# Attention and expansion kernel: DMA transposes from tile 8, two load buffers, a later model of the loads, and the last rows summed in two halves

## Chip, cores and metric

The kernel runs on one core of one Trainium2 chip. The metric is device microseconds of that core. A time is the median of several runs. A ratio is the mean time of one kernel's fast runs over that of the other kernel's fast runs in the same rounds, so it is not quite the ratio of the medians quoted.

## The reference

Attention with a sliding window of 96 keys, 8 global keys and a linear position bias, then a two-layer network with a squared ReLU:

```python
# q, k, v: (4, 8, 768, 64), normal draws times 0.1
scores = scale * np.matmul(q, k.transpose(0, 1, 3, 2)) + bias    # bias = -slope * distance
scores = np.where(keep, scores, -1e9)
a = softmax(scores)
x = np.matmul(a, v)            # as (3072, 512)
out = np.maximum(x @ w_in, 0)**2 @ w_out     # (512, 2048), (2048, 512)
```

## The kernel before

The 3072 rows are 24 tiles of 128. For each tile q and k are loaded, cast to bf16 on the way, transposed, multiplied to scores, and so on to x, which is transposed again (`xT`). Two tiles make a block for the two layers (`hT`, `hs`, `acc`). A small planner (class `Plan`) takes operations with costs, dependences and buffers, and decides in which order they are written. A tracker then sets the semaphores: **each access waits for those written before it that touch the same tile.** The loads that GpSimd issues take eight completion semaphores in turn, called lanes below; each load that lands adds 16 to its lane, so a wait for 64 is a wait for the lane's fourth load.

Three places matter. The load buffers are a ring indexed by the tile's number:

```python
JQK, JX = 10, 10          # from these tiles on, q/k and x are transposed by DMA
NQ, NKT = 10, 2 * TPB
qk_ring = [const([P, 2, d_model], BF16, f"qk_{i}") for i in range(NQ)]

def load_part(n, j):
    swdge(("qk"[n], j), qk_ring[j % NQ][:, n, :].rearrange(...),
          src_rows((q, k)[n], j).rearrange(...), 0.85)
```

The loads of tiles 1 to 5 and of all weights are written at once, ahead of the plan; those from tile 6 on are operations of the plan, which wait for the readers of their buffer:

```python
load_part(0, 1); ...; load_part(1, 1); load_v(0); load_v(1)
for w in "i0 T2 i1 T3 i2 o0 i3 o1 i4 o2 T4 i5 o3 i6 o4 T5 i7 o5 o6 o7".split():
    kind, n = w[0], int(w[1:])
    {"T": load_tile, "i": load_w_in, "o": load_w_out}[kind](n)
...
for j in range(NT):
    if j in late:                          # late = range(6, 24)
        ld = plan.op(("load", j), {"POOLQ": 2.6}, emit_load,
                     deps=qk_users[j % NQ] + [ones[j]], ...)
    ...                                    # transposes of tile j, reading qk_ring[j % NQ]
```

And all matmuls, transposes among them, go through TensorE in the written order.

The softmax here doesn't subtract the row's maximum and nothing guards it: scores larger than these inputs give would overflow.

## Time and profile before

| what | value |
|---|---|
| time | 221.83 us, 3 runs, 221.41 to 222.29 |
| span of the profile | 220.5 us |
| first transpose of tile 1's q starts | 5.70 us |
| TensorE's waits for loads of q and k | 4.0 us |
| last matmul ends / span ends | 216.45 / 220.5 us |

In the profile's lines PE is TensorE, PEld its weight loads, DVE VectorE, ACT ScalarE, POOL GpSimd and SP SyncE. The DMA share in the ten-microsecond windows can read above 1; use it only to compare rows. The prediction below shows the lines it rests on. Beside them, the page's row of slices: 40 equal slices of the span, busy tenths of TensorE, its granted clock in tenths, and the busy share of the DMA engines.

```profile
PE   7779879799999999999999999999999999999992
PEclk9979999999999999999999999999999999999998
DMA  9999999999999999999542532531730620310211
```

TensorE is nearly full from the ninth slice on, and its only holes are in the first 46 us, while the DMA engines are full.

### The profile page before, as it was taken

To read this page: it belongs to the slowest core of one execution; us is meant where nothing else is said; L and a number is where in the kernel's file an instruction comes from. 1 tells how busy PE (TensorE), PEld (TensorE's weight loads), DVE (VectorE), ACT (ScalarE), POOL (GpSimd) and SP (SyncE) were. 2 spreads that over 40 slices of the span, in tenths; PEclk is the share of its full clock that TensorE was granted. 3 is DMA by queue.
4 is the path that set the end of the run, shared out by engine and by line. 5 is a ranking of instruction groups with operands and counts; after the bars stand their busy time and mean duration, and the time that the engine had idled before them with its cause. 6 is when DMAs were issued, how large, how long until landed. Compare 5 with 4: busy or idle time off the path is not lost.

```text
span 220.5 us, 5058 instructions
## 1 busy us (share of the span) xinstructions
PE 206.9 (94%) x1992; PEld 143.5 (65%) x2024; DVE 144.0 (65%) x372; ACT 122.5 (56%) x224; POOL 73.7 (33%) x91
## 2 busy tenths in 40 slices
PE   7779879799999999999999999999999999999992
PEld 3658658457667676676667667666667766766740
DVE  5456858647677786775668668666767768745520
ACT  3648865626846657545636736733845744724430
POOL 7997658797962996404000000000000000000000
PEclk9979999999999999999999999999999999999998
DMA  9999999999999999999542532531730620310211
GB/s 129 148 167 200 180 190 192 165 208 161 165 189 131 155 199 145 158 197 132 140 60 48 144 54 45 147 64 33 168 72 4 166 27 12 109 24 16 82 38 59
DMA packets 107304, 26.03 MB, mean 118 GB/s; under 512 B 97936, under 2 KB 104336, under 8 KB 107280
## 3 DMA queue, kind: packets, MB, share of 16 engines
q0 software_dynamic: 79200, 13.37, 82.3%
q1 hardware_dynamic: 28080, 12.33, 25.7%
q8 instruction: 16, 0.26, 0.5%
q14 instruction: 8, 0.07, 0.1%
HBM read 27.26 MB, written 6.29 MB: 152 GB/s over the span
## 4 chain that ended last, share of the span: by engine, by line
PE 77%; DMA 12%; POOL 6%; issue 2%; DVE 1%; ACT 0%; POOLq 0%
PE hT L652 34%; PE acc L716 34%; DMA wout<-in_moe_w_out_dram 4%; PE sc L428 4%; DMA win<-in_moe_w_in_dram 4%; PE po L541 4%; DMA qk<-in_q_dram 4%; POOL qk L189 2%; POOL v L189 2%; POOL win L189 1%; PE tr L370 1%; POOL wout L189 1%; PE trx L604 1%; DVE hs L685 0%; ACT hr L673 0%
## 5 line engine op out<-in xcount | busy, mean ns | idle before, releaser
L652 PE MATMUL hT<-xT,win 128*128 128x256 bf16 x768 | 99.0, 273 | 0.2
L716 PE MATMUL acc<-wout,hs 128*128 128x512 bf16 x352 | 91.5, 379 | 2.0 <-DVE hs L685 0.6
L673 ACT ACTIVATE hr<-hT 128x512 f32<-128x512 f32 x96 | 57.3, 597 | 55.6 <-PE hT L652 54.1
L652 PEld LDWEIGHTS <-win 128*128 128x128 bf16 x768 | 71.1, 98 | 16.7
L685 DVE TENSOR_TENSOR hs<-hr 128x512 bf16<-128x512 f32 x96 | 65.0, 689 | 23.3 <-ACT hr L673 22.5
L716 PEld LDWEIGHTS <-hs 128*128 128x128 bf16 x384 | 36.6, 98 | 29.1 <-DVE hs L685 1.2
L474 ACT ACTIVATE esc<-sc 128x512 bf16<-128x512 f32 x78 | 42.3, 599 | 14.7 <-PE sc L428 14.7
L499 DVE TENSOR_TENSOR at<-esc,E 128x512 bf16<-128x512 bf16 x78 | 32.7, 421 | 8.6 <-ACT esc L474 7.2
L189 POOL DMA_DIRECT2D qk<-in_q_dram x23 | 20.8, 904 | 14.8 <-DMA qkT<-qk 9.0
L189 POOL DMA_DIRECT2D v<-in_v_dram x24 | 21.5, 896 | 7.6 <-DVE at L499 2.7
L189 POOL DMA_DIRECT2D qk<-in_k_dram x23 | 20.6, 897 | 2.8 <-DMA v<-in_v_dram 2.1
L569 DVE TENSOR_TENSOR x<-po,rs 128x256 bf16<-128x256 f32 x48 | 20.4, 424 | 1.7
L541 PEld LDWEIGHTS <-at 128*128 128x128 bf16 x352 | 16.7, 98 | 4.8
L541 PE MATMUL po<-v,at 128*128 128x65 bf16 x352 | 18.5, 193 | 0.0
L428 PEld LDWEIGHTS <-qkT 64*128 64x128 bf16 x352 | 10.0, 95 | 10.9 <-issue 8.0
L568 DVE RECIPROCAL rs<-po 128x4 f32<-128x4 f32 x48 | 8.5, 178 | 10.9 <-PE po L541 10.8
L428 PE MATMUL sc<-qkT 64*128 64x128 bf16 x192 | 13.4, 221 | 1.7 <-ACT qkT L300 0.9
L300 ACT COPY o<-acc 128x512 f32<-128x512 f32 (+1 forms) x15 | 8.4, 573 | 9.2 <-PE acc L716 8.3
L302 DVE COPY o<-acc 128x512 f32<-128x512 f32 (+1 forms) x10 | 6.6, 664 | 9.6 <-PE acc L716 5.0
L428 PE MATMUL sc<-qkT,qkT 64*128 64x128 bf16 x160 | 11.6, 218 | 0.0
L370 PE MATMUL tr<-ident,qk 128*128 128x128 bf16 x72 | 6.8, 225 | 4.0 <-DMA qk<-in_q_dram 2.1
L370 PEld LDWEIGHTS <-qk 128*128 128x128 bf16 x72 | 4.9, 101 | 6.1 <-DMA qk<-in_q_dram 3.0
(40 smaller groups left out, 72.9 us busy)
## 6 DMA issues: line engine op xcount, KB each, us to landing
out_dram<-o SPq DMA_DIRECT2D x23, 256.0 KB, 2.7
v<-in_v_dram POOLq DMA_DIRECT2D x24, 128.0 KB, 7.6
qk<-in_q_dram POOLq DMA_DIRECT2D x23, 128.0 KB, 7.4
qk<-in_k_dram POOLq DMA_DIRECT2D x23, 128.0 KB, 7.7
win<-in_moe_w_in_dram POOLq DMA_DIRECT2D x8, 256.0 KB, 8.1
wout<-in_moe_w_out_dram POOLq DMA_DIRECT2D x8, 256.0 KB, 8.8
plain<-in_q_dram SPq DMA_DIRECT2D x1, 256.0 KB, 3.2
plain<-in_k_dram SPq DMA_DIRECT2D x1, 256.0 KB, 3.9
```

Of the source, the lines that this page charges most:

```text
L189: nc.gpsimd.dma_start(out=dst, in_=src)
L370: nc.tensor.transpose(out=tr[:, pair, :], in_=src[:, pair * P : (pair + 1) * P], identity=ident32 if fp else ident,)
L428: nc.tensor.matmul(out=sc[odd, g][:, at, :], lhsT=qkT[(j - kt) % NKT][half, 1, pair, :], rhs=qkT[j % NKT][half, 0, pair, :], start=True, s ...
L474: nc.scalar.activation(out=esc, in_=tiles.pop(("sc", j, odd, g)).rearrange("p a c -> p (a c)"), func=Act.Exp, scale=scale,)
L499: nc.vector.tensor_mul(at, tiles.pop(("esc", j, odd, g)), bias)
L541: nc.tensor.matmul(out=po[:, hi, :], lhsT=tiles["at", j, odd, g][:, at * P : (at + 1) * P], rhs=v_sb[kj][:, h, :], start=(i == 0), stop=(i ...
L568: nc.vector.reciprocal(rs, po[:, :, D : D + 1])
L569: nc.vector.tensor_tensor(out=x[:, 4 * hf : 4 * hf + 4, :], in0=po[:, :, :D], in1=rs.to_broadcast([P, 4, D]), op=Alu.mult,)
L652: nc.tensor.matmul(out=hT[:, c, :], lhsT=w_in_sb[s][:, kt, c * P : (c + 1) * P], rhs=tiles["xT", blk][:, kt, :], start=(kt == 0), stop=(kt ...
L673: nc.scalar.activation(hr, tiles.pop(("hT", blk, s)), Act.Relu)
L685: nc.vector.tensor_mul(hs, hr, hr)
L716: nc.tensor.matmul(out=tiles["acc", blk, sub], lhsT=hs[:, c, sub * P : (sub + 1) * P], rhs=w_out_sb[s][:, c, :], start=(s == 0 and c == 0) ...
```

## The change

Its intent: less TensorE work (transposes of tiles 8 and 9 go to DMA), less memory (two load buffers, each load just in time), a planner that knows better when loads land, and a shorter end. Its core:

```diff
-    LAG = {..., "SP": 2.6, "POOLQ": 2.5, "DMA": 0.0}
+    LAG = {..., "SP": 2.6, "POOLQ": 0.8, "DMAQ": 1.2, "DMA": 0.0}
-    JQK, JX = 10, 10
-    NQ, NKT = 10, 2 * TPB
+    JQK, JX = 8, 8
+    NQ, NKT = 2, 2 * TPB
-        land[name] = issue[1] + 0.3
+        land[name] = issue[1] + 0.3 + min(max(0.1 * (issue[1] - 8), 0.0), 1.6)
+            ld = plan.op(("data", j), {"DMAQ": 2.7}, None, deps=[ld], key=base)
...
+        parts = [(0, None), (1, 0), (1, 1)] if last else [(0, None), (1, None)]
...          # the second half of the last rows has an accumulator of its own:
+                    pool, tag = (ps_g, "g") if own else (ps_acc, "acc")
+                    tiles["acc", blk, sub, half] = pool.tile([P, w], FP32, name="acc", tag=tag)
-                        rhs=w_out_sb[s][:, c, :],
+                        rhs=w_out_sb[s][:, c, cols],
...          # and both halves are copied out by ScalarE
```

More of the change, by code (lines that the diff above doesn't have):

```diff
@@ L22 @@
 class Plan:
-    LAG = {"PE": 0.25, "ACT": 0.15, "DVE": 0.12, "SP": 2.6, "POOLQ": 2.5, "DMA": 0.0}
+    LAG = {"PE": 0.25, "ACT": 0.15, "DVE": 0.12, "SP": 2.6, "POOLQ": 0.8, "DMAQ": 1.2, "DMA": 0.0}
     URGE = 0.05
@@ L701, with emit_s2 @@
         last = blk == NBLK - 1
-        acc_users = [[], []]
+        acc_users = {}
+        parts = [(0, None), (1, 0), (1, 1)] if last else [(0, None), (1, None)]
         order2 = (
-            [(s, sub) for sub in range(2) for s in range(NSTEP)]
+            [(s, *p) for p in parts for s in range(NSTEP)]
             if last
-            else [(s, sub) for s in range(NSTEP) for sub in range(2)]
+            else [(s, *p) for s in range(NSTEP) for p in parts]
         )
-        for s, sub in order2:
-            users = acc_users[sub]
-            def emit_s2(e, blk=blk, s=s, sub=sub):
+        for s, sub, half in order2:
+            users = acc_users.setdefault((sub, half), [])
+            w = d_model if half is None else d_model // 2
+            cols = slice(0, w) if half is None else slice(half * w, (half + 1) * w)
+            own = half == 1
+            def emit_s2(e, blk=blk, s=s, sub=sub, half=half, w=w, cols=cols, own=own):
                 if s == 0:
-                    tiles["acc", blk, sub] = ps_acc.tile([P, d_model], FP32, name="acc", tag="acc")
+                    pool, tag = (ps_g, "g") if own else (ps_acc, "acc")
+                    tiles["acc", blk, sub, half] = pool.tile([P, w], FP32, name="acc", tag=tag)
                 hs = tiles["hs", blk, s]
@@ L716, in emit_s2 @@
                     nc.tensor.matmul(
-                        out=tiles["acc", blk, sub],
+                        out=tiles["acc", blk, sub, half],
                         lhsT=hs[:, c, sub * P : (sub + 1) * P],
-                        rhs=w_out_sb[s][:, c, :],
+                        rhs=w_out_sb[s][:, c, cols],
                         start=(s == 0 and c == 0),
@@ L726 @@
             o = plan.op(
-                ("s2", blk, s, sub), {"PE": 0.43}, emit_s2,
+                ("s2", blk, s, sub), {"PE": 0.43 * w / d_model}, emit_s2,
                 deps=[d, land["wout", s]] + users[-1:],
-                key=8 * blk + s + 2.0 + (50 if last and sub else 0),
-                takes=("acc", NACC, [users]) if s == 0 else None,
+                key=8 * blk + s + 2.0 + (0 if not last else 8 * sub + 8 * (half or 0)),
+                takes=((*G, [users]) if own else ("acc", NACC, [users])) if s == 0 else None,
             )
@@ L734 @@
             if s == NSTEP - 1:
-                for half in (0, 1) if last and sub == 1 else (None,):
-                    cols = (
-                        slice(None)
-                        if half is None
-                        else slice(half * d_model // 2, (half + 1) * d_model // 2)
-                    )
-                    ousers = []
-                    def emit_o(e, blk=blk, sub=sub, half=half, cols=cols):
-                        o_sb = work.tile([P, d_model], FP32, name="o", tag="o", bufs=4)
-                        any_copy(e, o_sb[:, cols], tiles["acc", blk, sub][:, cols])
-                        tiles["o", blk, sub, half] = o_sb
-                    costs = {"ACT": 0.57, "DVE": 0.62}
-                    if half is not None:
-                        costs = [{"ACT": 0.4}, {"DVE": 0.35}][half]
-                    ev = plan.op(
-                        ("o", blk, sub), costs, emit_o, deps=[o], key=8 * blk + s + 1.0,
-                        takes=("o", 4, [ousers]),
-                    )
-                    users.append(ev)
-                    ousers.append(ev)
-                    def emit_st(e, blk=blk, sub=sub, half=half, cols=cols):
-                        r0 = (blk * 2 + sub) * P
-                        nc.sync.dma_start(
-                            out=out[r0 : r0 + P, cols],
-                            in_=tiles.pop(("o", blk, sub, half))[:, cols],
-                        )
-                    st = plan.op(
-                        ("st", blk, sub), {"SP": 0.4}, emit_st, deps=[ev],
-                        key=8 * blk + s + 9.0,
-                    )
-                    ousers.append(st)
@@ L772, with emit_o @@
-    for o in plan.run({"PE": 4.2, "DVE": 4.4, "ACT": 4.2}):
+                ousers = []
+                def emit_o(e, blk=blk, sub=sub, half=half, cols=cols):
+                    o_sb = work.tile([P, d_model], FP32, name="o", tag="o", bufs=4)
+                    any_copy(e, o_sb[:, cols], tiles["acc", blk, sub, half])
+                    tiles["o", blk, sub, half] = o_sb
+                ev = plan.op(
+                    ("o", blk, sub), {"ACT": 0.57, "DVE": 0.62} if half is None else {"ACT": 0.37},
+                    emit_o, deps=[o], key=8 * blk + s + 1.0, takes=("o", 4, [ousers]),
+                )
@@ new lines, with emit_st @@
+                users.append(ev)
+                ousers.append(ev)
+                def emit_st(e, blk=blk, sub=sub, half=half, cols=cols):
+                    r0 = (blk * 2 + sub) * P
+                    nc.sync.dma_start(
+                        out=out[r0 : r0 + P, cols],
+                        in_=tiles.pop(("o", blk, sub, half))[:, cols],
+                    )
+                st = plan.op(
+                    ("st", blk, sub), {"SP": 0.4}, emit_st, deps=[ev],
+                    key=8 * blk + s + 9.0,
+                )
@@ L773 @@
+                ousers.append(st)
+    for o in plan.run({"PE": 4.2, "DVE": 4.4, "ACT": 4.2, "DMAQ": issue[1]}):
         if o["emit"]:
```

## The prediction

> **What bounds the kernel now.** I read the ten-microsecond windows first, because the page's "PE 94%" is an average over stages. Columns: stretch, its length, then busy microseconds of TensorE, its weight loads, VectorE, ScalarE and GpSimd, the granted TensorE clock, the DMA share and GB/s.
>
> ```profile
> 0.00:10.00 10.00, 7.47 (x78) 4.65 (x79) 4.92 (x28) 4.57 (x8) 8.87 (x15) 1.00 1.37 137
> 10.00:20.00 10.00, 8.21 (x114) 6.91 (x113) 5.57 (x35) 6.03 (x14) 8.56 (x12) 0.83 1.87 178
> 20.00:30.00 10.00, 8.11 (x99) 5.68 (x100) 7.52 (x22) 7.56 (x17) 6.44 (x9) 1.00 1.63 189
> ...
> 50.00:60.00 10.00, 9.89 (x94) 6.93 (x94) 6.64 (x15) 6.90 (x14) 8.76 (x11) 1.00 2.43 156
> ```
>
> From about 46 us on every window but the last has 9.9 of 10 us busy on TensorE: whatever delays TensorE is added to the end, and only removed TensorE work is gained. Only the first 46 us have holes. The timeline of TensorE shows them: start, length, instruction, and in brackets the idle time and who ended it.
>
> ```profile
> 5.70 0.39 PE L370 MATMUL tr<-ident,qk 128*128 128x128 bf16 x4
> ...
> 11.90 0.40 PE L370 MATMUL tr<-ident,qk 128*128 128x128 bf16 x4 [1.01 <-DMA qk<-in_q_dram]
> 12.79 0.40 PE L370 MATMUL tr<-ident,qk 128*128 128x128 bf16 x4 [0.50 <-DMA qk<-in_k_dram]
> ...
> 26.36 0.39 PE L370 MATMUL tr<-ident,qk 128*128 128x128 bf16 x4
> 26.59 0.41 PE L541 MATMUL po<-v,at 128*128 128x65 bf16 x8
> 28.38 0.40 PE L370 MATMUL tr<-ident,qk 128*128 128x128 bf16 x4 [1.39 <-DMA qk<-in_k_dram]
> ...
> 42.73 0.40 PE L370 MATMUL tr<-ident,qk 128*128 128x128 bf16 x4 [1.10 <-DMA qk<-in_q_dram]
> ```
>
> The row at 5.70 is tile 1's q; the waits for loads add to 1.01 + 0.50 + 1.39 + 1.10 = 4.0 us. They come from the load queue, which GpSimd feeds in a fixed order; its timeline:
>
> ```profile
> 24.29 0.70 POOL L189 DMA_DIRECT2D wout<-in_moe_w_out_dram  x1 [0.57 <-DMA win<-in_moe_w_in_dram]
> 25.56 0.91 POOL L189 DMA_DIRECT2D qk<-in_q_dram  x1 [0.58 <-DMA wout<-in_moe_w_out_dram]
> 26.47 0.88 POOL L189 DMA_DIRECT2D qk<-in_k_dram  x1
> ...
> 34.40 0.91 POOL L189 DMA_DIRECT2D qk<-in_q_dram  x1 [0.58 <-DMA wout<-in_moe_w_out_dram]
> 35.30 0.88 POOL L189 DMA_DIRECT2D qk<-in_k_dram  x1
> ```
>
> The pair issued at 25.56 and 26.47 is tile 5. Each load reuses the completion semaphore of the one eight before it. So the issue at 34.40, for tile 6, had waited for the weight load issued at 24.29, and the issue at 35.30 found tile 5's q landed: that q landed between 34.1 and 35.3.
>
> The end, from the chain that ended last (start, length, what):
>
> ```profile
> 212.38 4.07 PE acc L716 x18
> 216.45 0.02 issue
> 216.47 0.38 ACT o L300
> 216.85 0.02 issue
> 216.88 0.42 DVE o L302
> ```
>
> The last rows are copied out in two halves one after the other, since both lie in one bank. Before 212.38 TensorE waited 0.55 us for the last square (in the timeline, "0.55 <-DVE hs L685").
>
> **What the Trainium skill says.** "DMA: Bandwidth & Descriptors", section "Why a DMA increments its semaphore by 16 and not by 1": only the full 16 means that the data has landed. That makes a wait value a count of loads, which I use below; no profile line shows a count. "TensorE: Matmul & The Clock Gate", section "What's actually happening": the array runs at half clock after an idle window of about 3.4 us and at full clock after a busy one. The trace agrees: eight warm-up matmuls of 512 columns take 3.21 us, 0.40 each, against 0.86 / 4 = 0.215 later, and after the gaps at 11 to 13 us the stretch 14.0 to 18.3 is granted 0.60. "PSUM — Partial Sum Buffer", section "PSUM bank collisions raise a hardware error": accesses of two engines to one bank must be kept apart by semaphores. The trace agrees in that VectorE's half starts 0.41 us after ScalarE's.
>
> **The change part by part.**
>
> *Transposes from tile 8.* Tiles 8 and 9 lose 8 TensorE transposes of q and k and 4 of x each: 24. Four take 26.59 - 26.36 = 0.23 us, so 24 x 0.0575 = 1.4 us less TensorE work. Six copies out of PSUM go too, off the path. The two extra DMA transposes of each kind cost no TensorE time.
>
> *Last rows.* The second half has its own bank, and its first half's sums fill the 0.55 us wait (in the new order four steps stand ahead of the step that needs the last square). The last copy no longer waits for its twin: 0.41 us. Together -1.0 us.
>
> *Loads modelled later.* Only order changes: transposes of tiles 2 to 7 move a few places.
>
> *Two load buffers.* This is the step that decides. The loads of tiles 1 to 5 are written into the program before any transpose, and they take buffer j mod 2. With ten buffers each tile had its own. With two, tiles 1, 3 and 5 share one, and 2 and 4 the other. The dependence tracker works in program order, so tile 3's and tile 5's loads find no reader to wait for, and tile 1's transposes, which come later, depend on the buffer's last writer: tile 5. I looked this up in the built program. Tile 1's q transpose waited for the first load of completion lane 0; now it waits for lane 1 at 64. Lane 1 carries tile 1's k, tile 3's q, a weight step and tile 5's q: 4 x 16 = 64, tile 5's q. Its k transpose waits likewise for tile 5's k. The issue order on GpSimd is unchanged through these loads, and none of them waits for TensorE.
>
> TensorE runs in order, and tile 1's q transposes stand right behind tile 0's: everything else is behind them. So TensorE stops at about 5.8 us and goes on when tile 5's q lands, about 34.7 (the middle of 34.1 to 35.3; at most slightly earlier, as the queue is limited by its own transfers, one per (34.7 - 16.2) / 16 = 1.16 us, taking tile 3's q as landed at 16.2 by the same lane argument).
>
> The sum: the row that stood at 5.70 stands at 34.7, +29.0. After it all of tiles 1 to 5 and nearly all weights are there, so of the 4.0 us of load waits I give back 3.0; the rest I expect to come back as the chain from scores to exponential to product, which these waits partly covered. The clock is cold at the restart, but the cold stretch 14.0 to 18.3 (about 0.40 x 4.3 = 1.7 us lost) should not come a second time: +0.5. Transposes -1.4, end -1.0. In all 29.0 - 3.0 + 0.5 - 1.4 - 1.0 = +24.1. On 221.83 that is 245.9, say 246.
>
> The loads of tiles 6 and later now wait for the transposes two tiles before. Between tile 4's last and tile 6's first transpose the new order holds about 15 us of TensorE work (seven groups of eight expansion matmuls at 0.87 and seven of sums at 0.86 make 12, attention the rest). Two issues at 0.9 us and some 4 us to land (3.1 is the least seen on these loads) fit, and for tile 8 another 3.3 us for the DMA transpose. I charge nothing.
>
> A side effect: tiles 1 to 3 compute with q and k of tiles 5 and 4. Scores are tiny beside the position bias (q and k are drawn at 0.1), so the result may still pass a tolerance; it is wrong all the same.
>
> **Rivals.**
>
> *The change as intended:* the overwritten buffers do not hold TensorE back. Then 4.0 us of load waits stay or shrink, -1.4 and -1.0 remain: about 219. For it speaks only that someone wrote it; the wait value speaks against it.
>
> *Loading just in time becomes a new wait.* With two buffers tiles 6 onward each wait for a free buffer. If a load with its transpose took over 15 us, each pair of tiles would lose some: nine pairs at 1 to 2 us would make 255 to 264. Against it: the profile's median of 7.4 us to landing is of a full queue, and the queue is empty after the restart.
>
> *The stall is shorter:* with VectorE and ScalarE idle the loads land sooner. GpSimd issues took 0.9 us, and the 26 loads ahead would need at least 26 x 0.87 = 22.6 us plus 3.1 to land, about 27 with the start. That would make 238. Against it: from 16 us on GpSimd itself waited for landings.
>
> *The restart is worse:* half clock for more than 4 us, as ScalarE's ten exponentials of 0.6 us starve TensorE. 2 to 4 us more: 248 to 250.
>
> **Range and chances.** The landing time is uncertain by 1.5 us, the given-back waits and the restart by 2 each, just-in-time loads only upwards: 241 to 251. A rival that leaves the time within 2% would need the wait value to be read wrongly. Faster 0.01, same 0.02, slower 0.97.
>
> **What would show it.** TensorE's timeline should have one gap of about 29 us before the second tile's transposes, ended by a q load, a clock near 0.5 for some 4 us after it; 99% busy again from about 70 us; 56 transposes of q and k in place of 72 and 32 of x in place of 40; GpSimd idle until tile 4's transposes; the last two copies both on ScalarE, the second alone at the end. Wrong would be: a gap that ends before 30 us, waits for loads of later tiles on TensorE, or no gap.

## The result

The changed kernel takes 245.16 us (4 runs, 244.62 to 245.87) against 221.66 us (the kernel before had four runs by then): ratio 1.1058, 95% interval 1.102 to 1.1095. It is slower by 23.5 us. The slices of its page:

```profile
PE   8000048999999999999999999999999999999994
PEclk9755557999999999999999999999999999999999
DMA  9999996009669997999998999699995951122202
```

TensorE does nothing in four slices of 6.07 us, and its clock is down to half in most of them and in the one after. The DMA engines are full through that time, as they were before; then they stand still, and later work in bits, since the loads now come just in time. TensorE's timeline around the hole:

```profile
4.58 1.56 PE L372 MATMUL tr<-ident,plain 128*128 128x128 f32 x8
33.63 0.61 PE L372 MATMUL tr<-ident,qk 128*128 128x128 bf16 x4 [27.49 <-DMA qk<-in_q_dram]
...
44.17 1.04 PE L654 MATMUL hT<-xT,win 128*128 128x256 bf16 x8
...
54.81 0.39 PE L372 MATMUL tr<-ident,qk 128*128 128x128 bf16 x4
...
71.66 0.61 PE L372 MATMUL tr<-ident,qk 128*128 128x128 bf16 x8
```

The row at 33.63 is tile 1's q transpose, which stood at 5.70 before: 27.93 us later, after one wait of 27.49 us for a load of q. The profile does not say which load. The built program does: the wait is for lane 1 at 64, tile 5's q, as the prediction has it. The timeline of GpSimd fits:

```profile
1.25 1.01 POOL L189 DMA_DIRECT2D qk<-in_q_dram  x1 [0.80 <-POOLq L789]
...
25.23 0.91 POOL L189 DMA_DIRECT2D qk<-in_q_dram  x1 [0.60 <-DMA wout<-in_moe_w_out_dram]
26.14 0.88 POOL L189 DMA_DIRECT2D qk<-in_k_dram  x1
...
31.71 0.70 POOL L189 DMA_DIRECT2D wout<-in_moe_w_out_dram  x1 [0.61 <-DMA win<-in_moe_w_in_dram]
55.05 0.91 POOL L189 DMA_DIRECT2D qk<-in_q_dram  x1 [22.64 <-PE trx L606]
```

The q issued at 25.23 is tile 5's, as in the kernel before (25.56). Tile 1's own q was issued at 1.25, 32 us before TensorE went on. After the last weight load GpSimd waits 22.64 us for tile 4's transposes, to load tile 6. The profile names a neighbouring transpose of x; the built program's wait is for those of tile 4.

The whole list of TensorE's waits begins so (who, for whom, total us, times, longest):

```profile
PE tr L372 <- DMA qk<-in_q_dram: 27.5, 1, 27.5
PE warm L250 <- DVE v L238: 1.2, 1, 1.2
PE sc L430 <- DVE qkT L303: 0.5, 1, 0.5
```

One wait for a load in the whole run. The windows answer to those of before:

```profile
10.00:20.00 10.00, 0.00 (x0) 0.00 (x0) 0.00 (x0) 0.00 (x0) 8.93 (x12) 0.50 1.85 175
...
30.00:40.00 10.00, 5.85 (x68) 4.71 (x68) 2.05 (x7) 2.17 (x4) 1.40 (x2) 0.51 1.52 180
40.00:50.00 10.00, 9.29 (x137) 7.05 (x135) 6.73 (x37) 9.14 (x21) 0.00 (x0) 1.00 0.02 4
...
60.00:70.00 10.00, 9.95 (x115) 7.36 (x113) 8.07 (x18) 6.86 (x13) 2.62 (x3) 1.00 0.71 47
```

And the end of the chain that ended last:

```profile
234.59 4.80 PE acc L724 x38
239.40 0.02 issue
239.42 0.37 ACT o L301
```

The last copy waits for no twin, and the sums run through without a wait.

### The profile page after: what moved, and what is told of

Its sections match the earlier page's. It is cut to its first block, busy times and chain, and to the rows that moved or that the text cites. A ratio compares the mean times of both kernels' runs of the same rounds, so it can differ in the third digit from the quotient of the medians.

```text
span 242.8 us, 5041 instructions
## 1 busy us (share of the span) xinstructions
PE 207.1 (85%) x1983; PEld 144.8 (60%) x2016; DVE 141.3 (58%) x367; ACT 121.0 (50%) x223; POOL 73.8 (30%) x91
## 4 chain that ended last, share of the span: by engine, by line
PE 81%; DMA 7%; POOL 6%; DVE 2%; issue 1%; ACT 1%; POOLq 0%
PE hT L654 35%; PE acc L724 33%; PE sc L430 6%; PE po L543 4%; DMA wout<-in_moe_w_out_dram 4%; DMA qk<-in_q_dram 3%; POOL qk L189 2%; PE sc L440 2%; POOL win L189 1%; POOL v L189 1%; PE tr L372 1%; PE trx L606 1%; POOL wout L189 1%; DVE x L571 1%; DVE hs L687 0%
## 5 line engine op out<-in xcount | busy, mean ns | idle before, releaser
L724 PE MATMUL acc<-wout,hs 128*128 128x512 bf16 (+1 forms) x367 | 91.0, 370 | 1.5
L724 PEld LDWEIGHTS <-hs 128*128 128x128 bf16 x400 | 38.5, 98 | 27.5 <-DVE hs L687 0.3
L372 PE MATMUL tr<-ident,qk 128*128 128x128 bf16 x56 | 5.4, 232 | 27.5 <-DMA qk<-in_q_dram 27.5
L303 DVE COPY qkT<-tr 128x512 bf16<-128x512 bf16 x6 | 2.5, 423 | 32.3 <-PE tr L372 32.1
L372 PEld LDWEIGHTS <-qk 128*128 128x128 bf16 x56 | 4.0, 104 | 28.5 <-DMA qk<-in_q_dram 27.7
L476 ACT ACTIVATE at<-sc 128x512 bf16<-128x512 f32 x10 | 5.4, 595 | 31.1 <-PE sc L440 31.1
L543 PE MATMUL po<-v,at 128*128 128x65 bf16 x352 | 19.0, 194 | 0.5 <-ACT at L476 0.3
```

What stands on the lines that cost most here:

```text
L372: nc.tensor.transpose(out=tr[:, pair, :], in_=src[:, pair * P : (pair + 1) * P], identity=ident32 if fp else ident,)
L476: nc.scalar.activation(out=esc, in_=tiles.pop(("sc", j, odd, g)).rearrange("p a c -> p (a c)"), func=Act.Exp, scale=scale,)
L543: nc.tensor.matmul(out=po[:, hi, :], lhsT=tiles["at", j, odd, g][:, at * P : (at + 1) * P], rhs=v_sb[kj][:, h, :], start=(i == 0), stop=(i ...
L724: nc.tensor.matmul(out=tiles["acc", blk, sub, half], lhsT=hs[:, c, sub * P : (sub + 1) * P], rhs=w_out_sb[s][:, c, cols], start=(s == 0 an ...
```

## The experiments

The theory: two buffers make the loads of tiles 3 and 5 overwrite tile 1's, and 4 overwrite 2's, before anything has read them; the tracker, which goes by the written order, makes tile 1's transposes wait for tile 5. The main rival: two buffers, with loads just in time, are too few.

| kernel | time, us | ratio to before (95% interval) |
|---|---|---|
| changed, own buffers for tiles 0 to 5 | 217.66 | 0.9813 (0.9789 to 0.9837) |
| changed, ten buffers | 218.32 | 0.9844 (0.9824 to 0.9865) |
| changed, five buffers | 217.67 | 0.9796 (0.9761 to 0.9831) |
| changed, four buffers | 244.84 | 1.1033 (1.1006 to 1.1061) |
| changed, three buffers | 238.41 | 1.0720 (1.0684 to 1.0757) |
| changed, two buffers, loads written in order | 218.07 | 0.9830 (0.9807 to 0.9854) |
| changed, idle matmuls in the wait | 243.57 | 1.0985 (1.0930 to 1.1040) |
| own buffers, DMA transposes from tile 10 | 218.49 | 0.9851 (0.9826 to 0.9876) |
| before, two buffers | 246.60 | 1.1113 (1.1092 to 1.1133) |
| before, DMA transposes from tile 8 | 221.85 | 0.9984 (0.9956 to 1.0012) |
| before, last rows in two halves | 219.97 | 0.9914 (0.9893 to 0.9935) |
| before, later model of the loads | 220.40 | 0.9938 (0.9915 to 0.9961) |

The kernel before ran beside them in three series, at 221.95, 222.22 and 221.70 us.

**Own buffers for the tiles that are loaded ahead.** Tiles from 6 on still share two.

```diff
-    qk_ring = [... for i in range(NQ)]
+    NOWN = NFIRST + 2                                   # 6
+    def slot(j): return j if j < NOWN else NOWN + j % NQ
+    qk_ring = [... for i in range(NOWN + NQ)]           # and slot(j) for j % NQ throughout
```

> The changed kernel, but tiles 0 to 5, whose loads are written ahead of every transpose, get a buffer each; tiles 6 and later still share two. Theory (overwritten buffers hold TensorE back until tile 5's q lands): the gap of 27.5 us before tile 1's transposes goes, the time falls by about 25 us to 218 to 220, under the kernel before. Rival (loading just in time is what costs): tiles 6 and later still load just in time, so it stays above 240. Mixed: between 222 and 235, if both cost.

217.66 us. TensorE's first waits in that run:

```profile
PE tr L377 <- DMA qk<-in_k_dram: 1.3, 3, 0.8
PE warm L255 <- DVE v L243: 1.2, 1, 1.2
```

The hole is gone, and with it 27.5 us against the changed kernel (1.1058 - 0.9813 = 0.1245, times 221). The time is a little under the range expected. Loading just in time is still there, so it is not the loss.

**Ten buffers.**

```diff
-    NQ, NKT = 2, 2 * TPB
+    NQ, NKT = 10, 2 * TPB
```

> The changed kernel with ten load buffers again, all else as changed. Theory: no tile of the first five is overwritten, so 218 to 220, the same as with own buffers for the first tiles within 1 us. Rival (just-in-time loading costs): this is faster than the run with own first buffers by several us.

218.32 us. The two intervals overlap, so ten buffers give nothing over two for the later tiles.

**Four buffers, and five.** The same line, with 4 and 5.

> The changed kernel with four load buffers: tiles 1 and 5 share one, 2, 3 and 4 have their own. Theory: tile 1's transposes still wait for tile 5's q, so the time stays at 244 to 246 although the buffers are doubled, with one gap of about 27.5 us on TensorE. Rival (too few buffers for the later tiles): doubling them gives back about half, 232 or less.

> The changed kernel with five load buffers: one more than the four that stalled, and tiles 1 to 5 all have their own. Theory: the whole loss goes, 217 to 220. Rival (a loss that shrinks gradually with the number of buffers): 240 or more.

Four: 244.84 us, as slow as two. The wait is the same:

```profile
34.31 0.61 PE L372 MATMUL tr<-ident,qk 128*128 128x128 bf16 x4 [28.45 <-DMA qk<-in_q_dram]
```

Five: 217.67 us. So doubling the buffers gave nothing and one more gave 27 us. With four, tiles 1 and 5 still meet; with five, none of the first five do.

**Three buffers.** Tiles 1 and 4 meet, and 2 and 5.

> The changed kernel with three load buffers: tiles 1 and 4 share one, 2 and 5 another, 3 has its own. Theory: the wait is for the last writer, whatever the number of buffers, so TensorE now has two gaps: tile 1's transposes start when tile 4's q lands (some 7 to 9 us before tile 5's, near 25), tile 2's only when tile 5's q lands (near 33.6). Only the work between the two, 6.7 us after the stall of the changed kernel, is done earlier: 238 to 241. Rival (the number of buffers as such): 240 to 246 with one gap.

238.41 us, with two waits on TensorE, each for the last writer of its buffer:

```profile
25.97 0.61 PE L372 MATMUL tr<-ident,qk 128*128 128x128 bf16 x4 [20.06 <-DMA qk<-in_q_dram]
...
33.71 0.61 PE L372 MATMUL tr<-ident,qk 128*128 128x128 bf16 x4 [0.29 <-DMA qk<-in_q_dram]
```

Tile 1 goes on when tile 4's q lands; the second wait, tile 2's for tile 5's q, is almost filled by the work between. This is the sharpest test: three buffers are faster than four, which no story of too few buffers allows.

**Two buffers, with the loads written in order.** The same loads in the same order on GpSimd, but as operations of the plan, each tile's load behind the transposes of the tile two before:

```diff
-    for w in "i0 T2 i1 T3 ...".split(): ...   # written at once
+        last_ahead = ahead[w] = plan.op(("ahead", w), {"POOLQ": ...}, lambda e: f(n),
+                                        deps=[last_ahead], key=-50.0)
+        d = plan.op(("data", w), {"DMAQ": ...}, None, deps=[last_ahead], key=-50.0)
...          # where tile j's transposes are made, j = 1 to 3:
+                ahead[f"T{j + 2}"]["deps"].append(tr)
```

> The changed kernel with its two load buffers kept, but the first loads and the weight loads are put into the plan, in the same order, each tile's load behind the transposes of the tile two before. So GpSimd issues the same loads in the same order, and the loads of tiles 3 to 5 wait for a reader. Theory (the order of writing, not the number of buffers, is what stalls): 217 to 220, no gap of over 2 us at the start. Rival (two buffers are too few in the first 40 us, when the load queue is full): the load of tile 3 or 5 waits for TensorE and holds all later loads back, 224 or more.

218.07 us. GpSimd waits once for a reader in that stretch, for tile 2's transposes before tile 4's load (start, length, idle time and releaser):

```profile
18.35 0.91 POOL L189 DMA_DIRECT2D qk<-in_q_dram  x1 [1.30 <-PE tr L385]
```

TensorE's longest wait for a load in that run is 1.2 us, for a weight. Two buffers are enough for the whole kernel, when the order of writing is right.

**The kernel before, with two buffers alone.**

```diff
-    NQ, NKT = 10, 2 * TPB
+    NQ, NKT = 2, 2 * TPB
```

> The kernel before with two load buffers and nothing else changed. Theory: the whole loss is here, and the gains of the other parts are missing: shift of the first transposes +27.9 us less some 3 us of load waits that the stall hides, 246 to 248. Rival (the order of the changed kernel, or its transposes by DMA from tile 8, takes part in the loss): under 240.

246.60 us, 24.65 more than the 221.95 of its rounds:

```profile
33.71 0.61 PE L370 MATMUL tr<-ident,qk 128*128 128x128 bf16 x4 [27.22 <-DMA qk<-in_q_dram]
```

TensorE goes on at 33.71, which is 28.01 later than before. So the one constant makes the whole loss, and 28.01 - 24.65 = 3.4 us come back later in the run.

**A warm clock through the wait.** 124 idle matmuls of 512 columns ahead of tile 1's transposes:

```diff
+                if (j, n) == (1, 0):
+                    busy = ps_acc.tile([P, 4 * P], FP32, name="busy", tag="acc")
+                    for i in range(124):
+                        nc.tensor.matmul(out=busy, lhsT=zero[:, :P], rhs=zero, start=True, stop=True)
```

> The changed kernel, stalled as it is, with 124 idle matmuls of 512 columns (zeros into an accumulator bank that is overwritten later) put ahead of tile 1's first transposes, to keep the clock up until tile 5's q lands. If the half clock after the stall costs: the stretch from 33.6 to 40 ran at 0.5, at most 3 us of it lost, some of that hidden behind the exponentials: 242 to 243.5. If it is hidden altogether: 244.5 to 245.5.

243.57 us. In the timeline:

```profile
5.71 26.93 PE L372 MATMUL busy<-zero 128*128 128x512 bf16 x124
34.15 0.40 PE L376 MATMUL tr<-ident,qk 128*128 128x128 bf16 x4 [1.51 <-DMA qk<-in_q_dram]
...
42.36 1.04 PE L658 MATMUL hT<-xT,win 128*128 128x256 bf16 x8
```

The granted clock was 1.00 here from 34.15 on. From tile 1's transposes to the first expansion matmul it took 42.36 - 34.15 = 8.21 us, against 44.17 - 33.63 = 10.54 in the changed kernel: by these two profiles the half clock costs 2.3 us. The load landed 0.5 us later in this run, so the spans differ by only 1.9. The median lies just above the range expected if the clock costs something, and the two intervals, 1.093 to 1.104 and 1.102 to 1.1095, overlap a little: the times alone do not show the gain clear of noise.

**The other parts, one at a time on the kernel before.** Each is the lines of the diff above that belong to it.

> The kernel before with transposes by DMA from tile 8 in place of 10 and nothing else. By the prediction's term: 24 transposes of 0.0575 us less on TensorE, 1.4 us, so 220.2 to 220.8; no more than 221.9 if the work given up was hidden, and more if the DMA transposes, now begun while the load queue is still full, make TensorE wait.

> The kernel before with only the last rows summed in two halves in banks of their own. By the prediction's term 1.0 us less (0.55 us of waiting for the last square, 0.41 of the two copies): 220.7 to 221.4. If only the copies count, 221.6.

> The kernel before with only the planner's model of the loads changed, so another order and nothing removed. The prediction charged nothing for it; the version with own first buffers is 4.3 us faster than before, of which 1.4 and 1.0 were to come from the other two parts, so about 1.9 us would be left for the order: 219.5 to 220.5. If the order is worth nothing: 221.5 to 222.5.

The later model alone gives 1.4 us (0.62% of 222): TensorE's waits for q and k fall from 4.0 to 1.9 us, although nothing was removed. 220.40 lies in the range expected, near its upper end. The two halves alone give 1.9 us, more than the 1.0 expected. The end of that run's chain:

```profile
210.27 4.80 PE acc L722 x38
215.07 0.02 issue
215.09 0.37 ACT o L300
```

From the last matmul to the end of the span are 218.2 - 215.07 = 3.1 us, against 220.5 - 216.45 = 4.05. Of these 0.9 us, 0.41 is the second copy; the rest is the last store, which takes 2.7 us from the end of the last copy, against 3.2 before. The other profiles bear this out: 3.2 to 3.4 us in the four without the two halves, 2.7 to 3.0 in eight of the ten with them. In the other two, own buffers and three buffers, it took 4.5 and 4.7; those were the slowest runs of their kernels. With the 0.55 us of waiting that makes 1.5; the other 0.4 us I can't place, and it is within the interval.

The transposes from tile 8 alone give 0.4 us, and the interval holds zero: under the 1.4 expected. TensorE's waits for q and k fell from 4.0 to 1.7 us in that run, but it has waits for weights and for a transpose by DMA, 2.1 us together, that the list of the kernel before does not have:

```profile
PE acc L716 <- DMA wout<-in_moe_w_out_dram: 1.4, 2, 0.9
PE tr L370 <- DMA qk<-in_q_dram: 1.3, 2, 1.0
...
PE hT L652 <- DMA xT<-x: 0.4, 1, 0.4
PE hT L652 <- DMA win<-in_moe_w_in_dram: 0.3, 1, 0.3
```

**The same part in company.** The version with own buffers, with the transposes by DMA from tile 10:

> The version with own buffers for tiles 0 to 5, with transposes by DMA from tile 10 again. By the prediction's term it does 1.4 us more TensorE work: 219 to 219.5. If the transposes by DMA from tile 8 give nothing, as the kernel before with only that part suggests (0.4 us), it is within 0.5 us of 217.7.

218.49 us against 217.66, or 0.84 us by the ratios (0.9851 - 0.9813, times 222). It lies between the two ranges expected. The two intervals overlap, so neither 0.4 nor 0.84 us is clear of noise. On the kernel before the interval leaves 1.0 us at most, less than the TensorE work removed; in company 1.4 is not excluded. How much went into the waits above is not settled.

## Why the prediction was right

The time, 245.16, lies 0.8 us from the 246 predicted. Step by step:

- **TensorE stops behind tile 0 and goes on with tile 5's q.** Right, and shown: the profile has the one wait of 27.49 us, and the runs with three, four and five buffers move or remove it just as the last writer of tile 1's buffer says. The landing was put at 34.7 and TensorE went on at 33.63, so the shift was 27.93 in place of 29.0. In other runs it was 33.71 to 34.31.
- **Load waits given back, 3.0.** All 4.0 us came back: the lists of both stalled kernels have no other load in them. By the pages TensorE's idle time outside the one wait fell by 4.7 us (220.5 - 206.9 = 13.6 before, 244.7 - 208.6 - 27.2 = 8.9 with two buffers alone). My fear that the waits would turn into waits of the attention chain was wrong: those come to 1.8 us in the changed kernel, between 36 and 56 us, and came to 1.7 in the kernel before.
- **Clock, +0.5.** Too small. At the restart 2.3 us went to the half clock, and no second cold stretch came (granted 1.00 from 40 us on). But the 1.7 us that the prediction set against it came from an unusual run. The profiled run of the kernel before had the half clock from 14.16 to 17.57 us and a mean granted clock of 0.989; of the 33 runs of this kernel in the three series only three have 0.990 or less. So most runs had no such stretch to give back. Nor does the stretch agree with the Trainium skill's "TensorE: Matmul & The Clock Gate", section "What's actually happening", as the prediction says: no idle window of 3.4 us came before it. TensorE was busy for 1.6 of the 3.4 us before, with no wait longer than 1.01.
- **Both together.** The net was to be 2.5 us back; with two buffers alone it was 3.4. How this divides between waits and clock is not settled.
- **Transposes, -1.4.** Too large on the kernel before (0.4, at most 1.0); 0.8 in company, where 1.4 is not excluded.
- **The end, -1.0.** Too small: 1.9 alone; the shorter last store was missed.
- **The later model of the loads, nothing.** Alone it is worth 1.4 us. In the stalled kernel it was not tested alone; it hardly can be worth that there, since what it removes is waiting for loads, and the stall has removed that already. The three other parts together were worth 246.60 - 245.16 = 1.4 us in the stalled kernel, or about 1.2 by the ratios, and 4.2 us with the stall mended (222 x 0.0187).
- **The sum.** In place of 29.0 - 2.5 - 2.4 = 24.1 the runs show 27.9 - 3.4 - 1.2 = 23.3, measured 23.5. That these agree tests nothing, since 3.4 and 1.2 were taken as differences of the same times. The three terms were off by -1.1, -0.9 and +1.2 us: the mechanism was right, but that the total came within 0.8 us is partly luck.
- **Loads just in time cost nothing.** Right: 16.9 us lie between tile 4's last transposes and tile 6's first (54.81 and 71.66), near the 15 counted in the order, and TensorE waits for no later load. One reading in that paragraph was wrong: 3.1 us is not the least time of these loads to landing but that of the DMA transposes, which the view by the tile `qk` mixes in. The least of the loads on GpSimd's queue was 4.3 in the kernel before and 3.3 in the changed one. The rival of a shorter stall, redone with 4.3, would have said 239 in place of 238.
- **What the profile was to show.** The gap (27.5 us, not 29), the half clock, TensorE full again before 70 us, 56 transposes of q and k and 32 of x, GpSimd idle until tile 4's transposes, and both last copies on ScalarE are there. The half clock held for 6.1 us, not 4.

Of the rivals, the change as intended (219), the shorter stall (238) and the long just-in-time loads (255 and more) did not come. A worse restart came in part, half clock for 6.1 us and 2.3 us lost to it, where the sum had a net 0.5; the waits given back paid for it.

The side effect is real. In the stalled versions some of tiles 1 to 3 are computed with the q and k of another tile, and they pass the comparison all the same. Working the reference through with the overwritten q and k of the changed kernel gives rows 128 to 511 that differ by 1.5% (norm of the difference over norm of the rows), at most 6.5e-5 where the largest output of these rows is 0.0038. Tile 4 is touched too, since its window reaches back to tile 3's keys: rows 512 to 606, 0.3% over the tile. No run shows this; it was worked on the host. The draws of q and k are so small that the position bias decides the weights. Passing a tolerance did not show that the right data was read.

What was to be gained is had by five buffers, by own buffers for the first tiles, or by two buffers written in order: 217.7 to 218.1 us, 1.7 to 2.0% under the kernel before, with intervals that lie below 1.

## What to carry to other kernels

Where a tracker like this one sets the waits, what counts is the order of writing: a second load written before the first one's reader binds that reader to the second load and to its data. Before shrinking a ring, ask for each slot which writes stand ahead of its first reader, and look up the wait value in the built program; that one number told of the stall in advance, while the number of buffers alone did not (three were faster than four). And a part that removes waiting can be worth little beside another that already removed it: the three other parts gave 4.2 us with the stall mended and 1.2 with it. Gains of parts measured one by one need not add up.

## What the Trainium skill lacked or had wrong

- "TensorE: Matmul & The Clock Gate", section "What's actually happening", gives one busy window, about 3.4 us sustained, until full clock. After the pauses here the clock stayed at 0.50 for 4.6 us (four buffers), 6.1 (changed kernel), 7.0 (the kernel before with two) and 9.1 (three). The page adds that the window is free-running, so a start inside one may take up to 6.8 us, an estimate from its 3.4; the last two are longer. The section does not say how full a window has to be. In the 3.4 us before the clock came back TensorE was busy for 2.9 to 3.4 us by the profiles, in the 3.4 us before those for 1.2 to 2.9. And it gives the half clock after an idle window, while the profile of the kernel before went to 0.50 after 3.4 us that were busy for 1.6.
- "DMA: Bandwidth & Descriptors", section "Measured (HBM→SBUF, 128 partitions, SWDGE, issued from GpSimd)", has 0.95 us for 64 KB, the transfer alone without the making of its descriptors, and I found no page with a figure for a queue of casting loads in short runs. Here a load of q (128 KB landed) took 7.4 us from issue to landing in the full queue (median; no load of that queue under 4.3), and 4.3 in the changed kernel after 50 us, where loads come just in time.
- No page has the effect that made this result: a buffer loaded again before its reader is written holds the reader until the last load (27.5 us), with wrong data and no error.
